# Seven block products of 256 columns for eight full ones in the second layer's feature transform, with right factors split one layer earlier

## The chip, the cores and the metric

The kernel runs on one core of a Trainium2 chip. The metric is the device time of one execution in microseconds; the kernel before was timed three times, and one more execution was profiled. The core's engines run side by side, each taking its own instructions in the order in which they were written: TensorE (PE: matmuls, with PEld its weight loads), VectorE (DVE), ScalarE (ACT), GpSimd (POOL) and SyncE (SP), whose queue starts the transfers (DMAs). They wait for each other by semaphores.

## The reference

Two layers, each an FNet block and an MLP block on x of 2048 rows (the sequence, S) by 512 features (D); all in fp32:

```python
a = jnp.einsum("bsd,ed->bse", x, dft_hid_re)
b = jnp.einsum("bsd,ed->bse", x, dft_hid_im)
y = jnp.einsum("ts,bse->bte", dft_seq_re, a) - jnp.einsum("ts,bse->bte", dft_seq_im, b)
...
h = _gelu(_layernorm(x, axis=-1) @ w1)
...
x1 = x + hs
h2 = _gelu(_layernorm(x1, axis=-1) @ w3) @ w4
return x1 + h2
...
x = x + _A_ref(_layernorm(x, axis=-1), A_dft_seq_re, A_dft_seq_im, A_dft_hid_re, A_dft_hid_im)
x = x + _B_ref(_layernorm(x, axis=-1), B_w1, B_w2, B_w3, B_w4)
```

The last two lines are done twice. `hs` in the MLP block is h, its four quarters shifted by one or two rows, times w2.

## The kernel before, in words

**Three matmuls for one.** Every fp32 operand is split into a high part, rounded to the matmul's format by ScalarE (a cast), and a low part, the difference, taken by VectorE. `mm3` (L294 to L297) multiplies high by high, high by low and low by high into one PSUM bank; only the third matmul of the three reads the low part of the left operand. So each operand costs a cast on ScalarE and a subtraction on VectorE ahead of TensorE.

**The FNet block.** The sequence transform is done first, in four chunks of 512 output rows (CH = 512, NC = 4), and its results re and im (the tiles `rr`, turned so that the features lie on partitions) are then multiplied by the 512 x 512 feature matrices `hs`. For a chunk c, TensorE goes through an x phase (`x_phase`, L499) and a y phase (`y_phase`, L528). In both, the sequence matrix comes in pieces of 512 KB through a ring. Item by item: SP loads a piece into a raw buffer (`issue_dma`, L223), `stage_one` makes the high part (L241 for a plain piece; L243 and L244, or L247 and L248, where two parts of it are first subtracted), `stage_two` (L258) makes the low part, and TensorE multiplies. The ring has four slots. `stream()` hands out the next item and, before that, stages the item three places ahead (`prefetch`); that one's slot is free only once TensorE has read the item four places before it.

The x phase has 16 items, two for each k from 0 to 7: a plain one with 12 matmuls (two `mm_half`) and a half one with 6. In chunks 1 to 3 the feature transform of the chunk before is woven in: eight further streams of `hs` pieces, at the k's that the list HAT names, each a call of `hid` with 12 matmuls of 512 columns into the two banks psd; four of them make two tiles of 128 rows. `add_y` (L596) then adds both banks to the rows of x (X0 or X1, in `tmp`) and takes their row sums, and `squares` (L337) on ScalarE sums the squares for the next norm.

**Work that is done late.** At the end of the y phase the results lie in PSUM and `tmp`. The sums and splits that make re and im of them are put off to the next x phase: `late` is a table from an item's number to functions, and `run_late(i)` issues those of item i just after the item's `stream()`. On VectorE these are additions (L492) and low parts (L453) of 128 x 1024 elements. The order in which they stand there, between the stream's own subtractions, is therefore written out by hand.

**The MLP block of layer 0.** It is done for two pairs of chunks. In the second pair (`by_pairs` from `c1, c2 = 2, 3`) five blocks of seven products each (`prod`, b1 to b7, six matmuls apiece) run through four banks of psd and psa; VectorE combines them (L492) and by that frees the banks, ScalarE applies gelu, and `w4_part` multiplies by w4 (12 matmuls). The loads are w3b (1.75 MB for a block, L845) and w4r (512 KB each, L833). Between them `one()` pops one step at a time from a list of background work (`bg`: norms and splits for layer 1).

## Time and profile before

| | us |
|---|---|
| three runs | 1418.74, 1419.22, 1419.19 |
| median | 1419.19 |
| profiled execution | 1418.97 |
| its span, first to last instruction | 1417.2 |
| TensorE busy | 1409.0 (99%) |
| VectorE busy | 1191.3 (84%) |
| ScalarE busy | 765.5 (54%) |

The span is 1.8 us shorter than the profiled execution. In a row of a group stand the line of the kernel, the engine, the operation, out<-in by the program's names, the shapes, the count, then busy time and mean duration of one in ns, and the idle time ahead of them with what ended it. In a timeline a row begins with start and duration in us, and a bracket at its end names the idle time ahead of it and who ended it. In windows the columns are busy times by engine with counts, TensorE's granted clock, the busy share of the DMA engines, and GB/s. A row on transfers gives the count, KB each, and the median from issue to landing in us. Matmuls overlap in TensorE's pipeline: their spacing, not their duration, is what one costs.

### The profile page before, as it was taken

How to read it: one execution, taken by the hardware profiler on the slowest of the kernel's cores; microseconds unless marked ns; L12 is line 12 of the kernel's file. 1: busy time of each engine (PE TensorE's matmuls, PEld its weight loads, DVE VectorE, ACT ScalarE, POOL GpSimd, SP SyncE). 2: the span in 40 equal slices, each digit the busy share in tenths (PEclk: the TensorE clock that was granted, in tenths of full speed). 3: DMA queues.
4: the chain of work that ended last, by engine and by line, in shares of the span. 5: the costliest groups of instructions: out<-in, count | busy, mean ns of one | idle time of the engine just before them, and what ended most of it. 6: DMA issues, size and time to landing. Idle time of an engine off the chain costs nothing.

```text
span 1417.2 us, 18479 instructions
## 1 busy us (share of the span) xinstructions
PE 1409.0 (99%) x6669; PEld 1181.8 (83%) x6669; DVE 1191.3 (84%) x1684; ACT 765.5 (54%) x1072; POOL 68.2 (5%) x105
## 2 busy tenths in 40 slices
PE   9999999999999999999999999999999999999998
PEld 8888788888788888988888888888888888899887
DVE  7988998998988789956789979879889788897776
ACT  6664555556566655534555545645555566454351
POOL 2100000000001100000000000000000020000000
PEclk9999999999999999999999999999999999999999
DMA  8978858778774748865556476565587457687864
GB/s 290 306 236 302 268 194 274 241 230 309 255 228 146 253 165 264 257 247 180 195 177 218 136 225 206 166 220 170 193 265 237 134 141 245 188 250 252 297 205 160
DMA packets 158907, 316.18 MB, mean 223 GB/s; under 512 B 10848, under 2 KB 78816, under 8 KB 156896
## 3 DMA queue, kind: packets, MB, share of 16 engines
q1 hardware_dynamic: 158816, 315.01, 67.9%
q8 instruction: 52, 0.85, 0.2%
q14 instruction: 39, 0.32, 0.1%
HBM read 260.70 MB, written 54.26 MB: 222 GB/s over the span
## 4 chain that ended last, share of the span: by engine, by line
PE 94%; DVE 3%; DMA 1%; ACT 1%; issue 1%; SPq 0%; POOL 0%; DVEq 0%; ACTq 0%; POOLq 0%
PE psd L295 10%; PE psd L296 10%; PE psd L297 10%; PE psa L295 8%; PE psa L297 8%; PE psa L296 8%; PE psb L296 7%; PE psb L297 7%; PE psb L295 7%; PE psc L295 6%; PE psc L296 6%; PE psc L297 6%; DMA raw<-in_ws 1%; DVE ring L258 1%; DVE rest L492 0%
## 5 line engine op out<-in xcount | busy, mean ns | idle before, releaser
L241 ACT CAST ring<-raw 128x1024 fp32r<-128x1024 f32 x127 | 132.9, 1052 | 69.4 <-PE psd L297 30.6
L258 DVE TENSOR_TENSOR ring<-raw,ring 128x1024 fp32r<-128x1024 f32 x126 | 153.4, 1220 | 14.3 <-ACT ring L241 14.3
L295 PE MATMUL psd<-ring,rr 128*128 128x512 f32 x208 | 80.9, 389 | 0.0
L296 PE MATMUL psd<-ring,rr 128*128 128x512 f32 x208 | 80.9, 389 | 0.0
L297 PE MATMUL psd<-ring,rr 128*128 128x512 f32 x208 | 80.9, 389 | 0.0
L248 ACT CAST ring<-ring0f 128x1024 fp32r<-128x1024 f32 x28 | 29.5, 1054 | 46.9 <-DVE ring0f L247 46.9
L258 DVE TENSOR_TENSOR ring<-ring1f,ring 128x512 fp32r<-128x512 f32 (+1 forms) x56 | 53.3, 952 | 0.8 <-ACT ring L244 0.7
L346 POOL TENSOR_TENSOR rows<-ve,mhalf 128x4 f32<-128x4 f32 x16 | 18.2, 1136 | 735.2 <-DVE ve L345 735.2
L295 PE MATMUL psc<-ring,ay 128*128 128x512 f32 x128 | 50.0, 391 | 1.6 <-ACT rr11f L518 1.6
L296 PE MATMUL psb<-ring,ay 128*128 128x512 f32 x128 | 50.0, 391 | 1.2 <-DVE ring L258 1.2
L297 PE MATMUL psb<-ring,ay 128*128 128x512 f32 x128 | 49.8, 389 | 0.0
L295 PE MATMUL psb<-ring,ay 128*128 128x512 f32 x128 | 49.8, 389 | 0.0
L296 PE MATMUL psc<-ring,ay 128*128 128x512 f32 x128 | 49.8, 389 | 0.0
L297 PE MATMUL psc<-ring,ay 128*128 128x512 f32 x128 | 49.8, 389 | 0.0
L297 PE MATMUL psa<-ring,ay 128*128 128x512 f32 x126 | 49.0, 389 | 0.0
L295 PE MATMUL psa<-ring,ay 128*128 128x512 f32 x126 | 49.0, 389 | 0.0
L295 PE MATMUL psd<-ring,ay 128*128 128x512 f32 x126 | 49.0, 389 | 0.0
L296 PE MATMUL psd<-ring,ay 128*128 128x512 f32 x126 | 49.0, 389 | 0.0
L296 PE MATMUL psa<-ring,ay 128*128 128x512 f32 x126 | 49.0, 389 | 0.0
L297 PE MATMUL psd<-ring,ay 128*128 128x512 f32 x126 | 49.0, 389 | 0.0
L314 POOL TENSOR_TENSOR rs<-ve,mhalf 128x2 f32<-128x2 f32 (+2 forms) x33 | 28.5, 863 | 412.4 <-DVE nb L313 393.4
L697 DVE TENSOR_TENSOR rg<-gt,rg 128x512 fp32r<-128x512 f32 x32 | 22.1, 690 | 29.6 <-ACT rg L696 29.6
(834 smaller groups left out, 4617.1 us busy)
## 6 DMA issues: line engine op xcount, KB each, us to landing
raw<-in_ws SPq DMA_DIRECT2D x183, 512.0 KB, 5.4
raw<-in_hs SPq DMA_DIRECT2D x56, 512.0 KB, 3.7
w3b<-w3d SPq DMA_DIRECT2D x11, 1792.0 KB, 8.5
w4r<-w4d SPq DMA_DIRECT2D x22, 512.0 KB, 3.5
un<-w4s SPq DMA_DIRECT2D x40, 256.0 KB, 3.7
un<-w4d SPq DMA_DIRECT2D x38, 256.0 KB, 4.4
x1d<-tmp SPq DMA_DIRECT2D x12, 512.0 KB, 6.8
xs<-x1d SPq DMA_DIRECT2D x12, 512.0 KB, 5.2
```

The source lines that it names most:

```text
L241: nc.scalar.copy(dest[:, a:b, 0], r[0][:, a:b])
L248: nc.scalar.copy(dest[:, :, 0], lo)
L258: nc.vector.tensor_tensor(lo, src, hi.bitcast(F32), op=ALU.subtract)
L295: nc.tensor.matmul(o, lh, rh, start=first, stop=False, skip_group_check=more)
L296: nc.tensor.matmul(o, lh, rl, start=False, stop=False, skip_group_check=more)
L297: nc.tensor.matmul(o, ll, rh, start=False, stop=last, skip_group_check=more)
L314: nc.gpsimd.tensor_tensor(rs[:, :n], ve[:, :n], mhalf[:, 0, :n], op=ALU.pow)
L346: nc.gpsimd.tensor_tensor(rs, ve, mhalf[:, :, :2], op=ALU.pow)
L697: nc.vector.tensor_tensor(lo, src, hi.bitcast(F32), op=ALU.subtract)
```

## The change

**In layer 1, for chunks 0 to 2, `hid` is no longer used.** The feature transform of a chunk is seen as a product of 2 x 2 blocks: the left matrix has the quarters a11, a21 (re, first and last 256 rows of the chunk) and a12, a22 (im); the right one has the left and right 256 columns of the real and imaginary feature matrix. Seven products of sums of blocks (left forms and right forms, numbered 1 to 7) replace eight. `form_product` does one: 4 x 2 x 3 = 24 matmuls of 256 columns into one bank of psd, then one VectorE addition of the bank to X0 or X1. The banks go on accumulating, so that the sums among products need no further addition. The products stand in the next chunk's x phase ahead of the items that FORMS names, in the order 1, 6, 5, 7, 3, 4, 2.

**Right forms.** The seven right forms are the same for all three chunks. They are made and split in layer 0, in the second pair of the MLP block: eight units (`right_unit`), each over 128 features and 128 columns of the blocks, with two loads, four additions, a cast of 7 x 128 elements, their lows, and stores in pieces of 512 B to a DRAM tile `hfd`. They run at the points where `one()` is called. In layer 1 a form of 1 MB, high and low parts, is loaded straight into a ring slot; such an item ("ready") has no cast and no subtraction.

**Left forms.** They are made in the x phase by `late`: additions, casts and lows. No im0 is split at the y phase's end any more. One raw buffer is kept free for form 3 from item 5 of the y phase up to item 12 of the x phase (`kept`). The row sums of X move from the additions to ScalarE (`row_sums`). Loads and stores of X and the norms and turns of the last chunk stand at other items.

```diff
+FORMS = {5: 1, 7: 6, 8: 5, 9: 7, 11: 3, 12: 4, 13: 2}
+RIGHT = (1, 6, 2, 3, 5, 7, 4)
...
             for k in range(NP):
-                if c:
+                if c and not layer:
                     for h in range(NP):
                         if HAT[h] == k:
                             item("plain", piece(hs[HORDER[h % 4]]))
                 p = piece(ws[c, k][:, 2:4])
-                item("plain", p)
-                item("one", p, span=(0, 1))
+                for i, kind in enumerate(("plain", "one")):
+                    if c and layer and 2 * k + i in FORMS:
+                        item("ready", FORMS[2 * k + i])
+                    item(kind, p, span=(0, 2 - i))
...
-                if (r < RAW or state["wide"] and i in y_pieces)
+                if (r < RAW - state["kept"] or state["wide"] and i in y_pieces)
...
+        if kind == "ready":
+            to = in_forms(dest).rearrange("p u h w -> p (u h w)")
+            nc.sync.dma_start(to.bitcast(F32), hfd[RIGHT.index(ids[0])].rearrange("p u h w -> p (u h w)"))
+            state["one"] += 1
+            return
...
+            if seven and 2 * k in FORMS:
+                form_product(c - 1, FORMS[2 * k])
-            while c and h < NP and HAT[h] == k:
+            while c and not seven and h < NP and HAT[h] == k:
...
+            if seven and 2 * k + 1 in FORMS:
+                form_product(c - 1, FORMS[2 * k + 1])
             s = stream()
             run_late(2 * k + 1)
...
+    def form_product(c, n):
+        s = in_forms(stream())
+        hi, lo, _ = left_forms[n]
+        bank = PD[n in (2, 5, 3)]
+        new = n in (1, 2, 5)
+        for u in range(4):
+            for q in range(2):
+                v = slice(q * P, (q + 1) * P)
+                first = new and u == 0 and q == 0
+                o = bank[:, q * 2 * P : (q + 1) * 2 * P]
+                mm3(o, hi[:, u, v], lo[:, u, v], s[:, u, 0], s[:, u, 1], first, True, not first)
...
+        add(x[:, :, v], bank.rearrange("p (q w) -> p q w", q=2), x[:, :, v])
...
+        if seven:
+            late.update(
+                {
+                    1: [lambda: add(im1s, im1s, re1s, ALU.subtract)],
+                    2: [lambda: add(re1s, re1s, t[:, 0:2]), lambda: add(re0s, re0s, t[:, 0:2])],
+                    3: [lambda: add(re0s, re0s, t[:, 2:4]), left_sum(7), left_high(1)],
+                    4: [lambda: add(im1s, im1s, X1), left_sum(5), left_low(1)],
+                    5: [left_sum(6), left_sum(3), left_high(6)],
+                    6: [left_low(6), left_high(5)],
+                    7: [left_low(5), left_high(7)],
+                    8: [left_low(7), left_high(3)],
+                    9: [left_low(3), left_high(4), left_high(2)],
+                    10: [left_low(4)],
+                    11: [left_low(2)],
+                }
+            )
+            return
...
+        starts = {0: 0, 2: 1, 5: 0, 7: 1, 10: 0, 12: 1, 15: 0, 20: 0}
...
+        def right_unit(u, n, x, highs_of):
...
+            k, v = u // 2, slice(u % 2 * P, (u % 2 + 1) * P)
+            if n == 0:
+                for r in range(2):
+                    src = hs[r, k // 2, :, k % 2].rearrange("p (b w) -> p b w", b=2)[:, :, v]
+                    nc.sync.dma_start(x[:, 2 * r : 2 * r + 2], src)
+            elif n == 2:
+                for o, a, b in ((4, 1, 0), (5, 3, 1), (1, 3, 4), (6, 2, 1)):
+                    add(x[:, o], x[:, a], x[:, b], ALU.subtract)
+                for f, hi in highs_of:
+                    nc.scalar.copy(hi.bitcast(F32R), x[:, f])
+            elif n == 3:
+                for f, hi in highs_of:
+                    add(x[:, f].bitcast(F32R), x[:, f], hi, ALU.subtract)
+                for f, t, r in ((slice(0, 7), x, 1), *((f, hi, 0) for f, hi in highs_of)):
+                    nc.sync.dma_start(hfd[f, :, k, r, v].rearrange("f p w -> p f w"), t)
+
+        def one():
+            if bg:
+                bg.pop(0)()
+            form_step()
...
-            x_phase(c, hook)
+            x_phase(c, hook, layer and c)
...
-            y_phase(c, hook)
+            y_phase(c, hook, layer and c < NC - 1)
```

Two places where the order moves. The first is VectorE early in the x phase of chunk 1 of layer 1. The names: `ring3f<-raw`, `ring_174<-raw` and their like are the stream's subtractions, rr11f and rr01f are im and re as sums, and rr_158, rr_160 their split tiles. Before:

```order
L243 TENSOR_TENSOR ring3f<-raw_180 128x512
L258 TENSOR_TENSOR ring_176<-raw_180,ring_176 128x2x512
L258 TENSOR_TENSOR ring_178<-ring3f,ring_178 128x512
L492 TENSOR_TENSOR rr11f<-rr11f,rr01f 128x2x512
L258 TENSOR_TENSOR ring_172<-raw_181,ring_172 128x2x512
L492 TENSOR_TENSOR rr01f<-rr01f,tmp 128x2x512
L243 TENSOR_TENSOR ring2f<-raw_182 128x512
L258 TENSOR_TENSOR ring_174<-raw_182,ring_174 128x2x512
L492 TENSOR_TENSOR rr11f<-rr11f,tmp 128x2x512
```

Now, from the fourth of these rows on (the rows ahead of it are the same; the line numbers have moved, L510 is the addition, L571 a left form's low, form7f the form of product 7, `rr_157<-rr0f,rr_157` the low part for product 1, and the last row the addition of product 1 to X0):

```order
L510 TENSOR_TENSOR rr1f<-rr1f,rr0f 128x2x512
L276 TENSOR_TENSOR ring_169<-raw_178,ring_169 128x2x512
L510 TENSOR_TENSOR rr0f<-rr0f,tmp 128x2x512 x2
L258 TENSOR_TENSOR ring2f<-raw_178 128x512
L510 TENSOR_TENSOR rr0f<-rr0f,tmp 128x2x512
L510 TENSOR_TENSOR form7f<-rr0f 128x1024
L276 TENSOR_TENSOR ring_173<-ring2f,ring_173 128x512
L510 TENSOR_TENSOR rr1f<-rr1f,tmp 128x2x512
L510 TENSOR_TENSOR rr0f<-rr0f,rr1f 128x4x256
L571 TENSOR_TENSOR rr_157<-rr0f,rr_157 128x4x256
L276 TENSOR_TENSOR ring_175<-raw_179,ring_175 128x2x512
L510 TENSOR_TENSOR tmp<-psd_248,tmp 128x2x256
```

Two additions and two forms have moved ahead of the first low part, and the addition of product 1 stands behind the low of one stream piece.

The second place is SP's queue at the start of the second pair of layer 0's MLP block: w3b and w4r are the weights' loads, cell and hx the inputs of the splitting units 0 and 1, hfd the stores of unit 0. Before:

```order
L845 DMA w3b_204<-w3d_80 128x3584
L833 DMA w4r_214<-w4d_102 128x1024
L833 DMA w4r_216<-w4d_92 128x1024
L833 DMA w4r_218<-w4d_93 128x1024
L833 DMA w4r_212<-w4d_94 128x1024
L833 DMA w4r_214<-w4d_95 128x1024
L845 DMA w3b_202<-w3d_81 128x3584
```

Now:

```order
L950 DMA w3b_201<-w3d_80 128x3584
L938 DMA w4r_211<-w4d_102 128x1024
L938 DMA w4r_213<-w4d_92 128x1024
L938 DMA w4r_215<-w4d_93 128x1024
L1171 DMA cell<-in_hs 128x2x128 x2
L938 DMA w4r_209<-w4d_94 128x1024
L1171 DMA hx<-in_hs 128x2x128 x2
L1181 DMA hfd<-cell 128x7x128
L1181 DMA hfd<-cell 128x5x128
L1181 DMA hfd<-junk 128x2x128
L938 DMA w4r_211<-w4d_95 128x1024
L950 DMA w3b_199<-w3d_81 128x3584
```

The units' loads stand among the weights' loads, and the stores of unit 0 ahead of the w3 load for the block after the next.

More of the change, by code (lines that the diff above doesn't have):

```diff
@@ L101, in spectral_mlp_kernel @@
     spare = at("spare", SPARE, 2, D, dtype=F32)
-    (re0, im0), (re1, im1) = ([both(f"rr{i}{h}", RR + (2 * i + h) * 4 * CH, 2, 2, CH) for i in range(2)] for h in range(2))
+    re_im = [both(f"rr{i}", RR + i * 8 * CH, KD, 2, CH) for i in range(2)]
+    (re0, im0), (re1, im1) = ([[t[:, 2 * h : 2 * h + 2] for t in pair] for pair in re_im] for h in range(2))
     rr = [[re0[0], re1[0]], [im0[0], im1[0]]]
@@ L191, in spectral_mlp_kernel @@
     for n, it in enumerate(items):
-        for i in it[1]:
+        for i in it[1] if it[0] != "ready" else ():
             uses.setdefault(i, []).append((n, "two" if it[0] == "plain" else "one"))
@@ L195, in spectral_mlp_kernel @@
     held = {i: None for i in range(len(raw_at))}
-    state = {"wide": False, "dma": 0, "one": 0, "two": 0, "use": 0, "made": 0, "done": 0, "limit": 0, "load": w_pieces[0]}
+    state = {"wide": False, "kept": 0, "dma": 0, "one": 0, "two": 0, "use": 0, "made": 0, "done": 0, "limit": 0, "load": w_pieces[0]}
     x_left = [(0, 1), (1, 1)] + [(j, 2) for j in range(2, NT, 2)]
@@ L254, in stage_two @@
         kind, ids, (a, b), _ = items[n]
+        if kind == "ready":
+            state["two"] += 1
+            return
         dest = slots[n]
@@ L497, in run_late, with x_phase @@
                 f()
-    def x_phase(c, hook):
+    def x_phase(c, hook, seven=False):
         h = 0
@@ L526, in x_phase @@
             nc.scalar.copy(re0s[:, i], PA[i])
-    def y_phase(c, hook):
+    quarters = [[t[:, :, :, i * 2 * P : (i + 1) * 2 * P] for t in pair] for pair in re_im for i in range(2)]
+    form3 = both("form3", RAWS + 6 * CH, KD, 2 * P)
+    form7 = both("form7", 5 * AY, 2, KD, 2 * P)
+    form6 = [both(f"form6{i}", word, KD, 2 * P) for i, word in enumerate((EXT + 4 * D, STG))]
+    a11, a21, a12, a22 = ((t[:, :, 0], t[:, :, 1], f[:, :, 1]) for t, f in quarters)
+    left_forms = {
+        1: a11,
+        2: a12,
+        3: (a11[0], *form3),
+        4: a22,
+        5: a21,
+        6: (form6[0][0], *form6[1]),
+        7: (form7[0][:, 0], form7[0][:, 1], form7[1][:, 1]),
+    }
@@ new lines, in left_high, with left_low, left_sum @@
+    def left_high(n):
+        hi, _, src = left_forms[n]
+        return lambda: nc.scalar.copy(hi, src)
+    def left_low(n):
+        hi, lo, src = left_forms[n]
+        return lambda: nc.vector.tensor_tensor(lo, src, hi.bitcast(F32), op=ALU.subtract)
+    def left_sum(n):
+        f = {i: v[2] for i, v in left_forms.items()}
+        o, a, b, op = {
+            7: (f[7], f[1], f[5], ALU.subtract),
+            6: (f[6], f[4], f[7], ALU.subtract),
+            3: (f[3], f[2], f[6], ALU.subtract),
+            5: (f[5], f[5], f[4], ALU.add),
+        }[n]
+        return lambda: add(o, a, b, op)
@@ new lines, in form_product, with row_sums @@
+    def form_product(c, n):
[9 more added lines that the diff above has]
+                mm3(o, hi[:, u, v], lo[:, u, v], s[:, u, 0], s[:, u, 1], first, True, not first)
+        left, right = slice(0, 2 * P), slice(2 * P, 4 * P)
+        to = {1: (X0, left), 2: (X0, left), 6: (X0, right), 3: (X0, right), 5: (X1, right), 7: (X1, right), 4: (X1, left)}
+        x, v = to[n]
+        add(x[:, :, v], bank.rearrange("p (q w) -> p q w", q=2), x[:, :, v])
+        if n in (2, 4):
+            j, known = c * TC + 2 * (n == 4), rows_sum()
+            def row_sums():
+                for i in range(2):
+                    nc.scalar.activation(junk, x[:, i], AF.Identity, accum_out=known[0][:, 0, i : i + 1])
+            at_mix = n == 4 and c == NC - 2
+            for key, f in (
+                ("y", row_sums),
+                ("y" if n == 4 else "y2", lambda: squares(known, [x[:, 0], x[:, 1]])),
+                ("10" if at_mix else "y+", lambda: y_stats(j, known)),
+            ):
+                late.setdefault(key, []).append(f)
@@ L529, in y_phase @@
+    def y_phase(c, hook, seven=False):
         for k, kind in y_order():
@@ L549, in y_phase @@
                         nc.scalar.copy(X1[:, i], PD[i])
-                    high(im0)
+                    if not seven:
+                        high(im0)
             else:
-                if k == NP - 2:
+                if k == NP - 2 and not seven:
                     low(im0)
@@ L1044, in by_pairs, with form_step @@
         bg += [lows("t4"), *early]
+        cell = at("cell", RAWS + CH, 12, P, dtype=F32)
+        of_hx, of_hc = (t.rearrange("p a (b w) -> p (a b) w", w=P) for t in (hx, hc[:, 6:8]))
+        rooms = (
+            (cell[:, 0:7], ((slice(0, 5), cell[:, 7:12]), (slice(5, 7), junk32))),
+            (of_hx[:, 0:7], ((slice(0, 7), of_hc[:, 0:7]),)),
+        )
+        starts = {0: 0, 2: 1, 5: 0, 7: 1, 10: 0, 12: 1, 15: 0, 20: 0}
+        points = {"n": 0}
+        def form_step():
+            for u, (start, room_of) in enumerate(starts.items()):
+                right_unit(u, points["n"] - start, *rooms[room_of])
+            points["n"] += 1
+        def right_unit(u, n, x, highs_of):
[18 more added lines that the diff above has]
+            form_step()
         bk, acc1 = mm4, acc4
@@ L1104, in by_pairs @@
         while bg:
-            one()
+            bg.pop(0)()
         def after_part(k):
@@ L1819, in hook @@
                 if c == NC - 1 and i == 12:
-                    for j in (0, 1):
+                    for j in (2, 3) if layer else (0, 1):
                         normed_act(tmp[:, j], xt(j), ln2[j])
-            x_phase(c, hook)
+            x_phase(c, hook, layer and c)
             def hook(k):
```

39 lines of the change are left out of this document (27 added, 12 removed).

## Prediction

> **What bounds the kernel now.** I read the page first: the engines' busy times, TensorE's clock, the chain.
>
> ```profile
> span 1417.2 us, 18479 instructions
> PE 1409.0 (99%) x6669; PEld 1181.8 (83%) x6669; DVE 1191.3 (84%) x1684; ACT 765.5 (54%) x1072; POOL 68.2 (5%) x105
> PEclk9999999999999999999999999999999999999999
> PE 94%; DVE 3%; DMA 1%; ACT 1%; issue 1%; SPq 0%; POOL 0%; DVEq 0%; ACTq 0%; POOLq 0%
> ```
>
> TensorE is busy for 99% of the span at full clock, and it is 94% of the chain. So taking matmuls away shortens the kernel one for one, and any new wait of TensorE lengthens it one for one. Everything hangs on whether the other engines still deliver in time. VectorE (DVE) is the next fullest. I therefore looked at one x phase with a feature transform in it (chunk 1 of layer 1) by windows, beside a stretch of layer 0 that multiplies in 256 columns only.
>
> ```profile
> core 0: us, PE busy (x) PEld busy (x) DVE busy (x) ACT busy (x) POOL busy (x), PEclk, DMA share, GB/s
> 797.40:851.80 54.40, 54.40 (x242) 45.05 (x241) 43.21 (x53) 27.22 (x35) 1.21 (x2) 1.00 0.65 200
> 570.00:590.00 20.00, 20.00 (x179) 20.00 (x178) 19.57 (x29) 11.98 (x18) 0.00 (x0) 1.00 0.82 256
> ```
>
> The x phase is 240 matmuls of 512 columns (16 items: eight of 12, eight of 6; eight feature streams of 12) in 54.40 us: 226.7 ns each, no gap. DVE has 11.2 us free in it, but only on average: DVE takes its instructions in the order written, so what counts is what stands ahead of one that TensorE needs.
>
> **The matmuls.** Removed per chunk: 96 of 512 columns. Added: 7 products x 24 = 168 of 256 columns. The price of the latter is in the stretch of layer 0, from one matmul to the twelfth after it:
>
> ```profile
> 572.05 0.28 PE L295 MATMUL psb<-un,hr 128*128 128x256 f32 x1
> 573.41 0.28 PE L295 MATMUL psb<-un,hr 128*128 128x256 f32 x1
> L295 PEld LDWEIGHTS psb<-un,hr 128*128 128x128 f32 x100 | 18.8, 188 | 0.1
> ```
>
> 1.36 / 12 = 113.3 ns, exactly half of 226.7. So 96 x 0.2267 = 21.76 us becomes 168 x 0.1133 = 19.04 us: -2.72 us per chunk, **-8.16 us** for three. A weight load lasts 188 ns by its own row, but successive loads overlap. [...]
>
> **The first product's left form.** The x phase begins on TensorE at 797.31. Before, the first feature stream stands after four items, at 805.47; after the change one more item of 12 matmuls (2.72 us) comes first, so product 1 is due at 808.19, and its third matmul, the first to read the low part of the left form, at 805.47 + 2.72 + 2 x 0.113 = 808.42. When is that low part there? These are DVE's rows of before at that place, and where TensorE stands:
>
> ```profile
> 797.31 0.39 PE L295 MATMUL psc<-ring,ax 128*128 128x512 f32 x1
> 805.47 0.39 PE L295 MATMUL psd<-ring,rr 128*128 128x512 f32 x1
> 797.51 0.69 DVE L243 TENSOR_TENSOR ring3f<-raw 128x512 f32<-128x512 f32 x1 [1.32 <-PE psa L297]
> 798.12 1.22 DVE L258 TENSOR_TENSOR ring<-raw,ring 128x1024 fp32r<-128x1024 f32 x1
> 801.36 1.23 DVE L258 TENSOR_TENSOR ring<-raw,ring 128x1024 fp32r<-128x1024 f32 x1 [0.28 <-ACT ring L241]
> 802.50 1.22 DVE L492 TENSOR_TENSOR rr01f<-rr01f,tmp 128x1024 f32<-128x1024 f32 x1
> 806.05 1.22 DVE L492 TENSOR_TENSOR rr11f<-rr11f,tmp 128x1024 f32<-128x1024 f32 x1
> 807.19 1.22 DVE L453 TENSOR_TENSOR rr<-rr01f,rr 128x1024 fp32r<-128x1024 f32 x1
> ```
>
> The row at 797.51 is decisive: DVE cannot run ahead, because that instruction waits for TensorE to leave the y phase (its ring slot), and all the rest stands behind it. Up to 802.50 the changed order is the same. From there it has eight more instructions up to the low part: a second addition to re, a 512-wide difference for the stream, the third addition, the form of product 7, a 512-wide low, the addition to im, the form of product 5, and then the low. An instruction of 1024 elements follows the next by 1.14 us (806.05 to 807.19), one of 512 by 0.61 us (797.51 to 798.12). So the low begins at 802.50 + 6 x 1.14 + 2 x 0.61 = 810.56 and ends 1.22 later, at 811.78. TensorE is due at 808.42: it **waits 3.36 us**. Nothing covers this: matmuls run in order, and the next items stand behind product 1. [...]
>
> **The next products.** The sum of each product into X reads PSUM, stands in DVE's queue right behind the product, and so holds DVE until TensorE is through; what the next product needs can only start then. An instruction like it, 512 elements from PSUM, is this row; I use 0.61 us as spacing:
>
> ```profile
> L596 DVE SCALAR_TENSOR_TENSOR tmp<-psd,tmp 128x512 f32<-128x512 f32 x24 | 16.3, 691 | 17.7 <-PE psd L297 17.7
> ```
>
> Product 6: TensorE has 1.36 + 2.72 us of stream items and 0.23 us of its own, 4.31 us, before it needs the low. DVE has the sum 0.61, a difference 0.61, two forms 2.28, a stream low 0.61, the low 1.22: 5.33. Wait 1.0 us. Product 5 comes one short item after it: 1.59 us of cover against the sum 0.61, a stream low 1.14, the low 1.22 = 2.97. Wait 1.4 us. Product 7 has 2.95 us against 2.44: none; products 3, 4 and 2 have 4 us and more of cover against 2.4: none. Together 5.8 us in each of three chunks, **+17.3 us**. Bounds: 3.36 alone, if what follows is absorbed (10.1 in all), and 8 per chunk (24) if transfers or restarts add to it.
>
> **Transfers of the right forms.** A ring slot becomes free when the item four places earlier has been read; at each of the seven products that leaves three items, 2.72 + 1.36 + 2.72 = 6.80 us, for 1 MB.
>
> ```profile
> w3b<-w3d SPq DMA_DIRECT2D x6, 1024.0 KB, 5.7
> zt0f<-zd SPq DMA_DIRECT2D x4, 1024.0 KB, 6.7
> ```
>
> Transfers of that size land in 5.7 to 6.7 us, and the order of SP puts each form ahead of the stream's own pieces, so I cost this at nothing; the cover is 0.1 to 1.1 us, plus the waits above, which lengthen it. What the stream saves (eight casts and lows per chunk) is off the path. In the y phase the row sums move to ScalarE (0.72 us each, four more per chunk); DVE waits for them once, about 1.5 us, against a lead of three items of 2.72 us: nothing. The moved loads, stores and turns of the last chunk keep a lead of several items: nothing.
>
> **Layer 0, second pair of chunks.** The eight splitting units add to DVE four 128-wide additions and 896 elements of lows each, to ScalarE 896 elements of casts, to SP five transfers with pieces of 512 B. DVE and ScalarE have the room. But DVE waits for the unit's input, and the banks of the hidden products wait for DVE.
>
> ```profile
> 613.40 0.32 SPq L833 DMA_DIRECT2D w4r<-w4d  x1
> w4r<-w4d SPq DMA_DIRECT2D x1, 512.0 KB, 9.3
> 616.20 0.69 DVE L492 TENSOR_TENSOR rest<-rest,psa 128x512 f32<-128x512 f32 x1 [0.59 <-PE psa L297]
> 617.49 0.69 DVE L492 TENSOR_TENSOR rest<-rest,psd 128x512 f32<-128x512 f32 x1 [0.60 <-PE psd L297]
> 620.93 0.69 DVE L492 TENSOR_TENSOR rest<-rest,psd 128x512 f32<-128x512 f32 x1
> 622.93 0.42 DVE L386 TENSOR_TENSOR ax0f<-tmp 128x256 f32<-128x256 f32 x1
> 624.09 0.39 PE L295 MATMUL psd<-b,w3b 128*128 128x512 f32 x1
> 527.54 3.08 SPq L642 DMA_DIRECT2D z3d<-z3turned  x4
> ```
>
> Unit 0's input is issued just ahead of the w4 load of 613.40, behind 1.8 MB of w3 and three w4 loads. That load lands 9.3 us after its issue, at 622.7; the unit's input, just ahead of it, I put at 622.2. In the new order its four additions (0.2 us each, from 0.42 for 256) stand between the rows of 616.20 and 617.49. So the four 512-wide sums that now run from 617.49 to 621.6 would end at 622.2 + 0.8 + 4 x 0.61 + 0.1 = 625.5. The last of them frees the bank that the matmul of 624.09 writes: wait 1.4 us. The same shape recurs in the next three of the five blocks, where the input stands behind a w3 load and 0.9 MB in 512 B pieces (about 3.6 us to issue, at 3.08 us for four 256 KB pieces like them): between 0 and 3.5 us each. I take 1.4 for each, as in the block with rows: **+5.6 us**, bounds 0 and 14. On SP the stores of a unit wait for DVE's lows, and behind them queues the next w3 load:
>
> ```profile
> w3b<-w3d SPq DMA_DIRECT2D x11, 1792.0 KB, 8.5
> ```
>
> It is needed one block later, 66 matmuls or 14.96 us, which leaves 6.5 us; the stores hold it for about 2 us of waiting and 3.6 of issuing. So it is hidden, barely; without that cover a block loses a microsecond or two, which the bound of 14 includes.
>
> **The sum.** The profiled execution took 1418.97 us (span 1417.2 and 1.8 around it), 0.22 below the median of 1419.19. 1418.97 - 8.16 + 17.3 + 5.6 = **1433.7 us**.
>
> **The rivals.** *Layer 0 hides its units* (their input lands in time, or the banks have more slack than I see): 1433.7 - 5.6 = 1428.1. For it: DVE is free for a third of that stage. Chance 0.29. *Only the first wait stays*, and the units are hidden: 1418.97 - 8.16 + 10.1 = 1420.9, no change. Against it: the orders of products 6 and 5 are as plain as that of product 1. 0.06. *The forms are ready in time* and it is faster: all of the waits go if DVE is at least 3.36 us earlier at product 1, 1410.8. For it: DVE has 11.2 us free in the phase. Against it: the wait at 797.51 pins DVE to TensorE, and from there it has one gap of 0.28 us. 0.07. *The 1 MB pieces decide*: if they land in 8.5 us, as w3's larger ones do, instead of within 6.8, the four products without a DVE wait lose 1.7 us each; since a wait lengthens the window of the next, I count three: 15.3 more, 1449.0. Against it: the two rows of 1 MB. 0.05. *The smaller products cost their weight load*: (168 x 0.188 - 21.76) x 3 = +29.5 for -8.16, 1471; the spacing of 113.3 ns speaks against it. 0.01. My forecast has 0.52.
>
> **The numbers.** The range takes in the forecast with its bounds in layer 0 and in the later products, and the first rival: 1422 to 1446. A measurement of this kernel can tell about 0.2% (2.8 us) from no change. Faster by more: 0.07. Within: 0.06. Slower: 0.87.
>
> **What would show it.** In the profile after: in the waits, TensorE for DVE at the first form's low, some 3.3 us in each of three x phases, then about 1.0 and 1.4 at products 6 and 5; x phases of some 57.5 us instead of 54.4; 256-column matmuls 113 ns apart; waits of TensorE for DVE between 624 and 680 us in layer 0, and DVE there waiting for the units' input. I am wrong if the phases are near 51.7 us without a wait at product 1, or if the waits are on transfers of forms.

## The result, and the profile after

The changed kernel takes 1491.28 us (median of 4 runs, 1489.38 to 1492.95) against 1419.2 us of the kernel before beside it: 1.051 times the time, 95% interval 1.0496 to 1.0522. That is 72 us slower, where 14.5 were forecast and 1446 was the upper end of the range. The page of its profile, the lines that stand against those shown of before, and then the view of the cores:

```profile
span 1490.5 us, 19040 instructions
PE 1427.0 (96%) x6885; PEld 1197.3 (80%) x6885; DVE 1207.0 (81%) x1723; ACT 762.9 (51%) x1094; POOL 98.8 (7%) x105
PE 75%; DVE 14%; DMA 4%; ACT 3%; issue 3%; SPq 1%; DVEq 0%; ACTq 0%
```

```profile
core 0: 1490.5 us, clock 0.987
```

VectorE now holds 14% of the chain instead of 3%, and TensorE's clock, 1.000 before, is 0.987 in the mean. TensorE is idle for 63.5 us of the span instead of 8.2. Its list of waits (engine, bank and line, for whom, us in total, times, the longest; rr0f is re and rr1f im as sums, `rest` a combination of products in layer 0's MLP block):

```profile
PE psc L313 <- DVE rr0f L510: 14.7, 2, 7.3
PE psd L313 <- DVE rr0f L510: 9.4, 5, 2.6
PE psd L313 <- DVE rest L510: 7.6, 3, 3.7
PE psd L315 <- DVE rr L571: 6.5, 6, 1.4
PE psa L313 <- DVE rest L510: 5.2, 2, 4.5
PE psd L313 <- DVE rr1f L510: 3.6, 2, 1.8
PE psd L315 <- DVE form L571: 3.1, 3, 1.2
...
PE psd L313 <- DMA ring<-hfd: 0.3, 1, 0.3
```

Three kinds stand there. The rows with psd for `rr0f`, `rr1f`, `rr` and `form` are layer 1's products and layer 0's x phases; those for `rest` are layer 0's second pair, with the units; and the longest, 7.3 us twice, is at a place that the prediction doesn't name. The next view shows the three x phases of layer 1 with the products, by windows:

```profile
836.20:897.98 61.78, 55.69 (x313) 48.49 (x312) 44.05 (x48) 20.66 (x26) 0.00 (x0) 0.97 0.66 225
941.61:1003.43 61.82, 55.76 (x313) 48.52 (x312) 44.05 (x48) 20.67 (x26) 0.00 (x0) 0.97 0.66 224
1047.05:1108.71 61.66, 55.75 (x313) 48.42 (x312) 44.06 (x48) 22.19 (x28) 0.00 (x0) 0.97 0.72 250
```

They last 61.7 to 61.8 us where they lasted 54.40 and where 57.5 were forecast; the clock in them is 0.97. VectorE has 17.6 to 17.8 us free in each and is late all the same.

From the starts of TensorE's matmuls (each spacing less 226.7 ns for 512 columns or 113.3 for 256, what is over 0.25 us taken as a wait, smaller surpluses over 40 ns as late starts) the whole can be laid out:

| part of the difference | us |
|---|---|
| seven products for eight streams, by the arithmetic of the prediction | -8.2 |
| 504 matmuls of the products start 120 ns apart, not 113.3 | +3.3 |
| the products wait (6.9, 6.9 and 6.7 in the three chunks) | +20.5 |
| layer 0's second pair, with the units | +16.0 |
| layer 0's x phases of chunks 1 and 2 (2.9 each) | +5.8 |
| the last four feature streams, after chunk 3 (8.3 in layer 0, 9.6 in layer 1) | +17.9 |
| the end of layer 0's chunk 3 | +0.8 |
| late starts behind these waits (19.4 us against 2.2) | +17.2 |
| sum; the spans differ by 73.3 | +73.3 |

Of the 19.4 us of late starts 13.9 lie where the granted clock is 0.50; the rest is mostly some 0.1 us at the matmul right behind a wait.

**The place that was not named.** These lines of the diff were not in the part on the change:

```diff
-    (re0, im0), (re1, im1) = ([both(f"rr{i}{h}", RR + (2 * i + h) * 4 * CH, 2, 2, CH) for i in range(2)] for h in range(2))
+    re_im = [both(f"rr{i}", RR + i * 8 * CH, KD, 2, CH) for i in range(2)]
+    (re0, im0), (re1, im1) = ([[t[:, 2 * h : 2 * h + 2] for t in pair] for pair in re_im] for h in range(2))
...
             s = stream()
+            if i == 1:
+                run_late("re0+", "re0++")
             hid(ri, dp, s, acc4, 0, i == 0, i == 3)
```

The four tiles re0, re1, im0 and im1 have become two, because a quarter (a11 and so on) runs over both halves. Memory and values are the same, but waits go by tile, as the next rows show. The two additions to re0 now also stand ahead of the second of the last four streams; they stood behind it. VectorE and then TensorE there, in layer 0:

```profile
402.73 1.23 DVE L471 TENSOR_TENSOR rr<-rr0f,rr 128x1024 fp32r<-128x1024 f32 x1
406.19 1.23 DVE L510 TENSOR_TENSOR rr1f<-rr1f,tmp 128x1024 f32<-128x1024 f32 x1 [2.24 <-PE psb L315]
408.58 1.23 DVE L471 TENSOR_TENSOR rr<-rr1f,rr 128x1024 fp32r<-128x1024 f32 x1 [1.17 <-ACT rr L468]
409.73 1.22 DVE L276 TENSOR_TENSOR ring<-raw,ring 128x1024 fp32r<-128x1024 f32 x1
410.86 2.48 DVE L510 TENSOR_TENSOR rr0f<-rr0f,beside 128x1024 f32<-128x1024 f32 x2
```

```profile
405.76 0.39 PE L315 MATMUL psb<-ring,rr 128*128 128x512 f32 x1
413.49 0.77 PE L313 MATMUL psc<-ring,rr 128*128 128x512 f32 x1 [7.33 <-DVE rr0f L510]
```

At 406.19 VectorE adds to im1 and has waited 2.24 us for TensorE, which was reading im0: the same tile now. The additions to re0 end at 413.3, and the second stream, which reads re1, starts at 413.49: it waited for re0, the same tile again. It needed neither.

**The clock.** Behind that wait the matmuls start 426 ns apart instead of 227. The windows of the wait, of what follows, and of the stretch after that:

```profile
405.90:413.40 7.50, 0.25 (x2) 0.00 (x0) 6.01 (x6) 3.07 (x4) 0.00 (x0) 0.86 0.54 186
413.50:418.00 4.50, 4.50 (x11) 3.54 (x12) 4.50 (x5) 4.50 (x6) 0.00 (x0) 0.50 0.35 133
418.00:424.00 6.00, 6.00 (x28) 4.96 (x27) 5.95 (x13) 3.03 (x4) 0.00 (x0) 0.99 0.24 80
```

For 4.5 us the granted clock is 0.50: 11 matmuls where 20 would fit. So this wait cost its length and about two microseconds more.

### The profile page after: what moved, and what is told of

Read it like the earlier page. It is cut to its first block, busy times and chain, and to the rows that moved or that the text cites. A ratio compares the mean times of both kernels' runs of the same rounds, so it can differ in the third digit from the quotient of the medians.

```text
span 1490.5 us, 19040 instructions
## 1 busy us (share of the span) xinstructions
PE 1427.0 (96%) x6885; PEld 1197.3 (80%) x6885; DVE 1207.0 (81%) x1723; ACT 762.9 (51%) x1094; POOL 98.8 (7%) x105
## 4 chain that ended last, share of the span: by engine, by line
PE 75%; DVE 14%; DMA 4%; ACT 3%; issue 3%; SPq 1%; DVEq 0%; ACTq 0%
PE psd L315 8%; PE psd L313 8%; PE psd L314 8%; PE psa L313 6%; PE psa L314 6%; PE psa L315 6%; PE psb L314 5%; PE psb L315 5%; PE psb L313 5%; PE psc L313 5%; PE psc L314 5%; PE psc L315 5%; DVE ring L276 3%; DMA cell<-in_hs 2%; DVE rr0f L510 2%
## 5 line engine op out<-in xcount | busy, mean ns | idle before, releaser
L256 ACT CAST ring<-raw 128x1024 fp32r<-128x1024 f32 x103 | 107.7, 1050 | 47.9 <-PE psd L315 17.4
L276 DVE TENSOR_TENSOR ring<-raw,ring 128x1024 fp32r<-128x1024 f32 x102 | 124.3, 1219 | 7.8 <-ACT ring L256 7.8
L364 POOL TENSOR_TENSOR rows<-ve,mhalf 128x4 f32<-128x4 f32 x16 | 49.2, 3076 | 756.2 <-DVE ve L363 756.2
L313 PE MATMUL psd<-ring,rr 128*128 128x256 f32 (+1 forms) x232 | 80.3, 346 | 13.6 <-DVE rr0f L510 9.4
L315 PE MATMUL psd<-ring,rr 128*128 128x512 f32 (+1 forms) x208 | 73.5, 353 | 6.5 <-DVE rr L571 6.5
L314 PE MATMUL psd<-ring,rr 128*128 128x256 f32 (+1 forms) x232 | 79.4, 342 | 0.0
L313 PEld LDWEIGHTS psd<-ring,rr 128*128 128x128 f32 x232 | 45.9, 198 | 22.2 <-DVE rr0f L510 9.1
L802 DVE TENSOR_TENSOR rg<-gt,rg 128x512 fp32r<-128x512 f32 x32 | 22.1, 690 | 44.7 <-ACT rg L801 44.7
L315 PEld LDWEIGHTS psd<-ring,rr 128*128 128x128 f32 x208 | 41.3, 199 | 12.2 <-DVE rr L571 7.7
L276 DVE TENSOR_TENSOR ring<-ring1f,ring 128x1024 fp32r<-128x1024 f32 (+1 forms) x50 | 49.2, 984 | 1.6 <-ACT ring L263 0.8
L510 DVE TENSOR_TENSOR tmp<-psd,tmp 128x512 f32<-128x512 f32 x21 | 14.5, 692 | 43.6 <-PE psd L315 43.6
L314 PEld LDWEIGHTS psd<-ring,rr 128*128 128x128 f32 x232 | 46.0, 198 | 4.5
```

The costliest lines, as they stand in the source:

```text
L256: nc.scalar.copy(dest[:, a:b, 0], r[0][:, a:b])
L276: nc.vector.tensor_tensor(lo, src, hi.bitcast(F32), op=ALU.subtract)
L313: nc.tensor.matmul(o, lh, rh, start=first, stop=False, skip_group_check=more)
L314: nc.tensor.matmul(o, lh, rl, start=False, stop=False, skip_group_check=more)
L315: nc.tensor.matmul(o, ll, rh, start=False, stop=last, skip_group_check=more)
L364: nc.gpsimd.tensor_tensor(rs, ve, mhalf[:, :, :2], op=ALU.pow)
```

## The experiments

### The joined tiles

**apart.** Two tiles for re and im in chunks 0 to 2 of layer 1 only, four elsewhere (the line that makes four tiles is put back, and the y phase chooses in the same way):

```diff
+    apart = [f[:, :, 1] for _, f in (re0, re1, im0, im1)]
+    joined = [f[:, 2 * h : 2 * h + 2, 1] for _, f in re_im for h in range(2)]
...
-    def x_phase(c, hook, seven=False):
+    def x_phase(c, hook, seven=False, to_forms=False):
+        re0s, re1s, im0s, im1s = joined if to_forms else apart
```

> re and im lie in four tiles again, as before the change, wherever no left forms are made (layer 0, and chunk 3 of layer 1); only chunks 0 to 2 of layer 1 use the two joined tiles. Theory of the joined tiles: an instruction on one half of a joined tile waits for instructions on the other half, and that alone makes the new waits in layer 0's x phases (1.95 + 0.95 us in each of two chunks), in the last hidden-layer streams of both layers (0.45 + 7.49 and 1.75 + 7.49 us) and about 0.8 us at the end of layer 0's chunk 3, together some 24 us, and with them some 5 to 6 us of TensorE at half clock right behind; so about 1462 us, between 1458 and 1466, and none of those waits left. Rival (the additions to re that now stand ahead of the second stream of the last four cause them): no change there, 1489 to 1493.

Measured: 1464.16 us (1461.32 to 1465.46), 27.1 less. The waits in layer 0's x phases and in the last streams of both layers are gone, and only those; the wait at the end of layer 0's chunk 3, which was expected to go too, is still there with 2.1 us. Of the list's rows for `rr0f`, 7.9 us in three products remain:

```profile
PE psd L313 <- DVE rr0f L512: 7.9, 3, 2.6
PE psd L313 <- DVE rest L512: 6.5, 3, 3.4
PE psd L315 <- DVE rr L574: 6.5, 6, 1.4
```

**adds_back.** The additions stand behind the stream again, the tiles stay joined:

```diff
-            if i == 1:
-                run_late("re0+", "re0++")
             hid(ri, dp, s, acc4, 0, i == 0, i == 3)
...
             if i == 1:
+                run_late("re0+", "re0++")
                 low(z_half(0, 0))
```

> The change is whole, but the two additions to re stand again behind the matmuls of the second of the last four streams, as before the change. Rival theory: their new place causes the 7.49 us waits, so both go, with the slow matmuls behind them: about 1491 - 2 x 7.5 - 4 = 1472 us. Theory of the joined tiles: what waits is the addition to im1, which writes a tile that the matmuls of the first stream still read, and it stands ahead of both; so the waits stay, or grow by up to a few us each since the additions now wait for one more stream: 1489 to 1500 us.

Measured: 1471.79 us (1470.1 to 1474.87), 19.5 less. So the theory of the tiles, as it stood, was wrong here and the rival right: both 7.49 us waits go. But the waits in layer 0's x phases stay (1.95 and 0.95 us, twice), which go with apart; the longer ones are this row:

```profile
PE psd L313 <- DVE rr1f L510: 3.6, 2, 1.8
```

The two runs together say that the long wait needs both: additions issued ahead of the stream, and a tile that they share with what the stream reads. Undoing either ends it; the rest of the 27 us is the tiles alone.

### VectorE's order in layer 1

**low_first.** Only the table of late work is changed:

```diff
-                    3: [lambda: add(re0s, re0s, t[:, 2:4]), left_sum(7), left_high(1)],
-                    4: [lambda: add(im1s, im1s, X1), left_sum(5), left_low(1)],
-                    5: [left_sum(6), left_sum(3), left_high(6)],
-                    6: [left_low(6), left_high(5)],
-                    7: [left_low(5), left_high(7)],
+                    3: [lambda: add(re0s, re0s, t[:, 2:4]), left_high(1), left_sum(7)],
+                    4: [left_low(1), lambda: add(im1s, im1s, X1), left_sum(6), left_sum(3), left_high(6)],
+                    5: [left_low(6), left_sum(5), left_high(5)],
+                    6: [left_low(5)],
+                    7: [left_high(7)],
```

> The change is whole, but VectorE makes the first product's low part before the addition to im and before the form of product 5, makes the forms of products 6 and 3 while product 1 runs, and has the low part of product 5 ready before product 6 ends. Theory of VectorE's order: product 1 waits about 1.2 us instead of 3.70, products 6 and 5 not at all instead of 1.36 and 1.58, so 5.4 us less in each of three chunks, 16 in all, and 4 to 6 us of half clock behind these waits go with them: 1469 to 1476 us. Rival (the products wait for transfers of their forms): the waits stay, 1488 to 1493.

Measured: 1480.58 us (1479.18 to 1481.28), 10.7 less: the right direction, two thirds of the least that was expected. Product 1 still waits 2.0 to 2.3 us, and a new entry is in the list, 2.1 us for the transfer of a form.

**forms_later.** A similar table, and the products later: `FORMS = {7: 1, 8: 6, 9: 5, 10: 7, 11: 3, 12: 4, 13: 2}`.

> The change is whole, but products 1, 6 and 5 stand one or two items later (items 7, 8, 9, 10, 11, 12, 13 in place of 5, 7, 8, 9, 11, 12, 13), and VectorE makes the low part of 1 ahead of the addition to im, the forms and low parts of 6 and 3 before product 1 ends. Theory of VectorE's order: no form's low part is late any more, 6.6 us less in each of three chunks and the 5 us of half clock with them, 1491.3 - 25 = 1466 us, if the 1 MB transfers land within their 6.8 us. If the transfers are what comes next, as the 2.1 us of waits for them in the order with the early low part suggest, each chunk keeps 1 to 3 us: 1469 to 1475 us. Rival (order is not the cause): 1488 to 1493.

Measured: 1482.74 us (1479.91 to 1483.06), 8.5 less where 16 to 25 were expected. Product 1 no longer waits. But each chunk has a wait of 1.2 us for a low part of the ring and one of about 3.1 us at product 6. There the form's transfer, issued only once a raw buffer ahead of it on SP had been freed by VectorE, landed as VectorE was done (836.78 us for the one, 836.85 for the other, with product 6 at 837.03, in the version all_three below). The profile puts it down to VectorE; the order of VectorE reaches the products through SP's queue too.

### The units in layer 0

VectorE, SP's queue and TensorE in the second of the five blocks, after the change:

```profile
658.12 0.69 DVE L510 TENSOR_TENSOR rest<-rest,psa 128x512 f32<-128x512 f32 x1
663.78 0.72 DVE L510 TENSOR_TENSOR cell<-cell 128x128 f32<-128x128 f32 x2 [4.97 <-DMA cell<-in_hs]
```

```profile
650.58 0.44 SPq L950 DMA_DIRECT2D w3b<-w3d  x1
653.97 0.37 SPq L1181 DMA_DIRECT2D hfd<-hx  x1
654.39 0.85 SPq L1181 DMA_DIRECT2D hfd<-hc  x1
655.28 5.45 SPq L1171 DMA_DIRECT2D cell<-in_hs  x2
```

```profile
664.55 0.39 PE L315 MATMUL psd<-bt,w3b 128*128 128x512 f32 x1
669.47 0.79 PE L313 MATMUL psa<-bt,w3b 128*128 128x512 f32 x1 [4.53 <-DVE rest L510]
```

The unit's two loads stand behind w3's 1.8 MB and the stores of the unit before, take 5.45 us to issue, and end VectorE's wait at 663.78; the sums that free TensorE's bank stand behind the unit's additions.

**no_units.** The step `form_step()` is taken out of `one()`, and layer 1 loads from `w4s`, other prepared weights of the same size.

> Work left out: the eight units that split the right forms in layer 0 are not run, and layer 1 loads its 1 MB forms from other prepared weights of the same size. Theory of the late unit inputs: the waits of TensorE between 642 and 735 us go (2.15 + 0.84 + 4.69 + 0.37 + 3.82 + 2.07, and 2.05 at its end, 16.0 us) and some 3.6 us of half clock with them: about 1471 us, 1468 to 1475. If the units cost only what the prediction said, 5.6 us: 1485.

Measured: 1471.26 us (1469.81 to 1471.76), 20.0 less: the units cost 20 us where 5.6 were forecast.

**units_ahead.** The unit's step changes places with w3's load:

```diff
-            w3_load(NF // 2 + p + 2)
-            one()
+            form_step()
+            w3_load(NF // 2 + p + 2)
+            if bg:
+                bg.pop(0)()
```

> The change is whole, but the step that loads a unit's input stands ahead of the next w3 load on SP instead of behind it (in each of the five blocks). Theory: the input is late because the w3 load ahead of it waits until TensorE has read the w3 block that it overwrites, and then 1.8 MB land ahead of it; so VectorE's waits of 5.0 to 6.5 us for the units' input (4 times, 22.1 us in all) shrink to under 2 us in all but the first block, and TensorE's waits of 4.69, 3.82 and 2.07 us go with the half clock behind them (3.6 us): about 1477 us, 1474 to 1481. Rival (the input is late because its own 512 B pieces queue behind the stores of the unit before): the waits stay, 1488 to 1493.

Measured: 1485.59 us (1483.57 to 1490.06), 5.7 less and not 14. Its waits in that stretch:

```profile
DVE cell L510 <- DMA cell<-in_hs: 5.3, 1, 5.3
PE psa L313 <- DMA w3b<-w3d: 5.0, 2, 2.8
PE psa L313 <- DVE rest L510: 3.5, 3, 2.6
```

VectorE's waits for the input, 22.1 us in four after the change, are gone but for the first, so the cause of their lateness was named rightly. TensorE now waits for w3, which stands behind the units.

**act_loads.** `nc.sync.dma_start` becomes `nc.scalar.dma_start` for the units' loads.

> The change is whole, but ScalarE issues the loads of the units' input, so that they neither queue behind w3's and w4's loads on SP nor hold w3's load up. Theory of the late unit inputs: VectorE's waits for the input (22.1 us) fall below 4 us, and no wait for w3 takes their place, so most of the 16 us of TensorE's waits between 642 and 735 us and 3.6 us of half clock go: 1472 to 1478 us. If the transfers themselves are what is scarce (16 DMA engines shared with w3's 1.8 MB), the input still lands 5 us late, and the time stays above 1484.

Measured: 1489.72 us (1485.49 to 1491.16), within the noise of the change's own. Median times to landing there, and VectorE's wait:

```profile
cell<-in_hs ACTq DMA_DIRECT2D x10, 128.0 KB, 9.6
w3b<-w3d SPq DMA_DIRECT2D x4, 1792.0 KB, 10.4
```

```profile
DVE cell L510 <- DMA cell<-in_hs: 15.1, 6, 3.2
```

Side by side both are slow: 9.6 us for 128 KB, which took 7.9 on SP, and 10.4 for w3, which took 9.9. VectorE's waits for the input fell only from 22.1 to 15.1 us, so the queue was not the whole of it. The DMA engines that both queues feed were busy for 0.77 of the stretch from 600 to 745 us in this run, where before it was 0.58 of 600 to 740, and for 0.9 or more from 655 to 661 us. That they are what is scarce there fits this; no run tests it alone.

### Together, and what is left

**all_three** is apart, forms_later and units_ahead in one.

> All three together: four tiles where no forms are made, the later products, the unit's load ahead of w3's. If the three causes are separate, their gains add: 1491.3 - 27 - 25 - 14 = about 1425 us, 1420 to 1432; without any wait of the change's own it would be 1411. If one of them only moves a wait elsewhere, it stays above 1440.

Measured: 1449.11 us (1447.4 to 1452.42), 42.2 less than the change; the three alone gave 27.1 + 8.5 + 5.7 = 41.3. So the gains add up. The sum that was expected rested on larger single gains: two of the three mendings had, by themselves, only moved part of a wait, to w3's load and to product 6.

**all_three_b** has the units' loads on ScalarE, the products at `{7: 1, 9: 6, 10: 5, 11: 7, 12: 3, 13: 4, 14: 2}`, and a table to match.

> Four tiles where no forms are made; the units' loads issued by ScalarE; the products at items 7, 9, 10, 11, 12, 13 and 14, so that two items lie between product 1 and product 6, with the form and low part of 6 and 3 made before product 1 ends, and the form of product 7 ahead of the high part of product 1. Theory of three separate causes: layer 1's phases come to 52 to 53 us without a wait over 1 us, layer 0's units cost under 5 us: 1491.3 - 27 - 25 - 16 = 1423, minus what is left of the clock, 1414 to 1426. If the 1 MB transfers bind in the later places as well, 2 to 4 us in each chunk come back: 1426 to 1436.

Measured: 1452.18 us (1448.85 to 1452.81), above both of the ranges expected. In layer 1 VectorE no longer holds any product, and transfers do: the first row is from TensorE's waits, the second from the transfers of the first such phase, where the same row read 5.6 us after the change itself.

```profile
PE psd L313 <- DMA ring<-hfd: 11.5, 13, 2.3
```

```profile
ring<-hfd SPq DMA_DIRECT2D x7, 1024.0 KB, 7.5
```

**half_forms, rest_no_units, ceiling.** The same version with half of each form's bytes; with no units (and the units' queue as it was); and with both.

> Work left out: as the version with all three mended and the later products, but each right form is loaded by half (512 KB in place of 1 MB; the rest of the ring slot holds old values). Theory of the transfers: once VectorE's order is mended, products wait for their 1 MB (11.5 us in 13 waits); with half the bytes these waits go, 1452 - 11.5 - 1 to 3 us of half clock = about 1438 us, 1435 to 1442. Rival (something else holds the products, and the transfer only ends with it): 1448 to 1453.

> Work left out: as the version with all three mended and the later products, but layer 0's eight units are not run and layer 1 loads other prepared weights of the same size. The units' share in that version is 12 us of TensorE's waits between 624 and 715 us and 4 to 5 us of half clock: 1452 - 16 = about 1436 us, 1433 to 1439. If layer 0 with the units had cost only the predicted 5.6 us: 1446.

> Work left out: both of these (no units, half of each form's bytes), with four tiles where no forms are made and the later products. What is left of the change is its arithmetic: 2.72 us less of matmuls in each of three chunks. Theory (the matmul term of the prediction holds, and all of the loss is waits and the half clock behind them): 1419 - 8.2 = 1411 us, plus at most 8 us of small waits: 1411 to 1419. If products of 256 columns cost more than half of those of 512 in this phase (by their weight loads, say), it stays above 1425.

Measured: 1437.17 us (1436.83 to 1438.64), 15.0 less; 1432.4 us (1430.66 to 1434.32), 19.8 less; and 1420.34 us (1419.35 to 1422.26), 1.001 of before (1.0001 to 1.0019). The transfers and the units are what is left of the loss. But with both away the change is still no gain: 1420.34 is above the 1411 to 1419 that was expected, and below the 1425 of its rival. Two things remain in that profile. TensorE waits 1.25 us in each chunk for a low part of the ring (the row gives its idle time alone), and the products' matmuls start 120 ns apart.

```profile
PE psc L314 <- DVE ring L276: 3.3, 3, 1.1
```

**ceiling_order, ceiling_ring.** Two other orders of the late work for that wait. The first puts the form of product 7 and the split of product 1 one item later. The second puts the form of product 3 and the low part of 6 behind the ring's low part, and the form of product 5 one item later:

```diff
-                    6: [left_sum(6), left_high(6), left_sum(3), left_low(6)],
-                    7: [left_sum(5), left_high(5)],
-                    8: [left_high(7), left_low(5)],
+                    6: [left_sum(6), left_high(6)],
+                    7: [left_sum(3), left_low(6)],
+                    8: [left_sum(5), left_high(5), left_high(7), left_low(5)],
```

> Work left out as in the ceiling version; the form of product 7, the high and the low part of product 1 stand one item later, behind the ring's own low parts. Theory (the wait of 1.25 us per chunk for a ring's low part is VectorE's order): it goes, with the slower clock behind it, 1420.3 - 5.7 = about 1414.6 us, 1413.5 to 1416.5, which is faster than the kernel before by 0.2 to 0.35%. Otherwise 1419 to 1421.

> Work left out as in the ceiling version (no units, half of each form's bytes); the forms' instructions that stood ahead of the ring's low part for the long item behind product 1 (the form of product 3, the low part of 6) now stand behind it, and the form of product 5 one item later. Theory (that wait is VectorE's order): it goes in all three chunks, with the slower clock behind it: 1420.3 - 5.7 = about 1414.6 us, 1413.5 to 1417, faster than before by 0.1 to 0.35%. Otherwise 1419 to 1421.

Measured: 1423.68 us (1421.44 to 1427.11), where the wait grew to 1.93 us; and 1416.93 us (1415.45 to 1417.81), 0.9983 of before (0.9974 to 0.9992), where it is gone. So it was VectorE's order, but not the instructions that I first took. With the units and half of the transfers left out the change is worth 1.7 us. The matmuls alone, at 120 ns, would give 4.9; in that profile TensorE's waits and late starts are 3.7 us longer than before.

**all_three_c** is all_three_b with that order, nothing left out.

> Nothing left out: the version with all three mended, later products and the units' loads on ScalarE, with the same order of VectorE as the run beside it. If the transfers hold the products anyway, the new order saves little of 1452: 1447 to 1453 us. If the waits add, 5.7 less: about 1446.

Measured: 1449.76 us (1449.68 to 1451.16), 1.0218 of before (1.0204 to 1.0231). This is the case that was expected if the transfers hold the products anyway. No complete version had a median below 1449; the kernel before stays faster than all of them.

**half_by_half, one_moving, no_low_weights.** One execution each, for the 120 ns: the loops over halves and blocks exchanged; `s[:, 0, 0], s[:, 0, 1]` for all blocks; `hi` in place of `lo`.

> Work left out as in the ceiling version; a product goes through one half of its bank and then the other (12 matmuls each) instead of changing halves every three matmuls. If the changes of half cost the 6.7 ns, matmuls of a product start about 113 to 115 ns apart; otherwise 120 as before.

> Work left out as in the ceiling version, and each product multiplies the first block of its right form throughout in place of its four blocks. If reading the moving operand from changing places costs the 6.7 ns, matmuls start 113 ns apart; otherwise 120.

> Work left out as in the ceiling version, and each product uses the high part of its left form where it used the low part. If loading weights from two places costs the 6.7 ns, matmuls start 113 ns apart; otherwise 120.

Measured: 120.1, 120.1 and 120.3 ns in the mean, 119.9 in ceiling. None of the three is the cause by itself. In ceiling_ring, from one matmul of a product to the twelfth after it, 1.43 us:

```profile
834.50 0.28 PE L313 MATMUL psd<-ring,rr 128*128 128x256 f32 x1
835.93 0.28 PE L313 MATMUL psd<-ring,rr 128*128 128x256 f32 x1
```

What makes it 119 here and 113.3 in layer 0 stays open; that the operands lie in other tiles than in layer 0 was not varied.

## Why the prediction was wrong, step by step

**The bound** was right: every wait of TensorE lengthened the kernel. It was not one for one, though: late starts behind the waits added 17 us to their 61, 14 of them at the lower clock. The prediction has no term for that; "restarts" stand only in its bound of 24 us.

**The matmul term** was mis-sized: -8.16 us by 113.3 ns a matmul, about -4.9 by the 120 ns that the products show.

**The first product's left form** was right. The low part was to be begun 13.05 us after VectorE's first row of the phase and began 13.45 after it (849.85 against 836.40); the wait was to be 3.36 us and was 3.70 by the starts (2.78 + 0.92), in two pieces, whose idle times these rows give:

```profile
849.87 0.38 PE L313 MATMUL psd<-ring,rr 128*128 128x256 f32 x1 [2.62 <-DVE rr0f L510]
851.13 0.39 PE L315 MATMUL psd<-ring,rr 128*128 128x256 f32 x1 [0.76 <-DVE rr L571]
```

Already the first matmul waits, for the form of product 5 in the other half of the columns, the joined tile once more; the third, for the low part, would have ended the wait at the same time. **The next products** were right as well: 1.0 and 1.4 forecast, 1.0 to 1.4 and 1.6 measured, none at the others but for 0.3 to 0.5 us at one. The term of 17.3 us measured 20.5.

**Transfers of the right forms, "at nothing"**: true in the change, where 0.3 us of TensorE's waits are theirs, but by the cover of VectorE's lateness. Once that is mended they take 11.5 us. The rival of the 1 MB pieces, given 0.05, is what stands next in line.

**Layer 0, "I take 1.4 for each, as in the block with rows"**: the step that was mis-sized. The mechanism is the one named, an input that lands behind w3 and is waited for by VectorE, ahead of the sums that free the banks. In the first block TensorE waited 2.15 + 0.84 us. In the next three it is 5.1, 3.8 and 2.1 us, since there the loads stand behind a w3 load and the 512 B pieces at once, and VectorE waits 5.0 to 6.5 us for them. With 2.05 us at the stage's end these are 16.0 us, over the bound of 14, and 20 with the clock.

**The missing step** is the largest: 23.7 us of waits and their share of the clock, 27.1 in all by the run apart, come from the tiles that were joined and from additions issued one stream earlier. The sum of the prediction has nothing for layer 0's x phases and the last four feature streams of both layers; it costed the instructions in the places that the change means, and took re and im as they were. Without this step the time, 1464.16 us in apart, would still lie above the range, by layer 0's units and the clock above all. (The 0.8 us at the end of layer 0's chunk 3 are not of this: that wait is 0.8 to 2.2 us in the versions without the joined tiles there, and 1.3 us before.) The prediction should have asked of each tile whose bounds change who else touches it.

**The ranges.** The rivals had one mechanism each, and none held two of these terms at once. The upper end of 1446 is below even the sum of the prediction's own upper bounds (1418.97 - 8.16 + 24 + 14 = 1448.8), and has nothing for a term not seen.

## What to carry to other kernels

When a change redraws tiles, go through every reader and writer of the old tiles, also in phases that the change doesn't mean: here waits went by tile, two halves that were independent became one, and the cost fell on places far from the edit (7.33 us at a time). In a kernel whose bound engine is 99% busy, price a wait as its length plus the clock that it loses (here 61 us of waits and 14 at the lower clock behind them), and price a new stream of bytes in the phase where it must land, not by a transfer's time in another (1 MB landed in 5.7 to 6.7 us before, in 7.5 in all_three_b). A saving of 0.6% in arithmetic leaves no room for any of this; a version with the suspected costs left out, run first, shows the ceiling.

## What the runs showed of the hardware

After idle time TensorE's clock was granted at 0.50 for a few microseconds (4.5 us behind the wait of 7.33 us above). Much shorter waits did it too. Here 1.95 us were enough, at the end of layer 0's chunk 3, while waits of 1.79 us in layer 0's x phase and of 1.99 us in its MLP block were followed by full speed:

```profile
363.08 0.50 PE L314 MATMUL psb<-ring,ay 128*128 128x512 f32 x1 [1.95 <-DVE ring L276]
203.13 0.47 PE L313 MATMUL psd<-ring,rr 128*128 128x512 f32 x1 [1.79 <-DVE rr1f L510]
644.62 0.50 PE L313 MATMUL psd<-b,w3b 128*128 128x512 f32 x1 [1.99 <-DVE rest L510]
```

So the length of the wait alone didn't decide it here. In the record of the granted clock of the change's profile eight stretches stand at 0.50 ahead of the span's end, five of 3.41 us and three of 6.83, and all of them start and end on one grid of 3.41 us. By the windows of that grid the three waits differ (the first two rows belong to the first wait, the next two to the second, the last three to the third):

```profile
360.05:363.46 3.41, 1.46 (x7) 0.90 (x6) 2.80 (x3) 1.04 (x1) 0.00 (x0) 1.00 0.97 392
363.46:366.88 3.42, 3.42 (x10) 2.65 (x9) 3.42 (x6) 1.33 (x2) 0.00 (x0) 0.51 0.64 165
199.66:203.07 3.41, 1.68 (x8) 1.06 (x6) 3.05 (x4) 1.53 (x3) 0.00 (x0) 1.00 0.95 341
203.07:206.49 3.42, 3.36 (x15) 2.84 (x16) 3.09 (x4) 2.26 (x3) 0.00 (x0) 1.00 0.45 145
639.95:643.36 3.41, 2.68 (x12) 1.88 (x10) 2.48 (x7) 1.06 (x3) 0.00 (x0) 1.00 0.56 196
643.36:646.78 3.42, 2.16 (x9) 1.80 (x10) 2.69 (x5) 2.24 (x4) 0.00 (x0) 1.00 0.00 0
646.78:650.19 3.41, 2.73 (x12) 1.97 (x11) 3.34 (x9) 1.53 (x3) 0.00 (x0) 1.00 0.54 157
```

The first wait left 1.46 us of busy TensorE in its window, and the next window ran at half clock. The second left 1.68 us. The third, the longest, fell across the border of two windows and left 2.68 and 2.16 us. Among the windows at full clock of that profile, away from its start and end, eight were followed by one at 0.50: all seven in which TensorE was busy for less than 1.47 us of the 3.41, none in which it was busy for more than 1.77, and of the six between (1.48, 1.62, 1.68, 1.68, 1.69 and 1.77 us) the last. So where a wait fell on the grid counted here as well as its length.
